# A list scheduler that repeats its pass, maxima spread through DRAM, and a search that moves from ScalarE to VectorE

## The chip, the cores and the metric

The kernel runs on one core of a Trainium2 chip. The time of a run is the device time of the whole program in microseconds (us). TensorE (PE in the rows) multiplies matrices, VectorE (DVE), ScalarE (ACT) and GpSimd (POOL) work on tiles, SyncE (SP) issues nearly all DMAs. Each engine works through its own list of instructions in order; semaphores join the lists.

## The reference

Two independent parts, put side by side in the output (S = 2048 rows, D = 1024):

```python
# A: sliding-window attention, 32 heads of 32, window 256
qkv = x @ wqkv                                   # (S, 3 D)
scores = where(0 <= i - j < 256, q k^T / sqrt(32), -1e9)
a = (softmax(scores) @ v) @ wo
# B: Fourier mixing by given matrices
re, im = xb @ dft_hid_re.T, xb @ dft_hid_im.T
b = dft_seq_re @ re - dft_seq_im @ im
out = concatenate([a, b], axis=-1)               # (S, 2 D)
```

All arrays are float32.

## The kernel before

A float32 operand is divided by a power of two taken from its largest magnitude and split into two float16 halves, high by ScalarE and low by VectorE (`split`, L431 and L439; L1102 and L1103 for the cosine parts). Three float16 products (`PASSES`) stand for one float32 product. Most products are two by two block products in seven multiplications instead of eight (`seven`, `seven_parts`), whose block sums VectorE and GpSimd form (`summed`, L1076). A `seven` multiplies into the PSUM banks `m0` to `m3` and calls a hook after each of its parts; ScalarE copies its first product to a second bank (L1194).

The work in the order in which it is written down: the projections to q, k and v (`plan`: `plain_units`, `sum_unit`), through DRAM to attention; then 64 units (`units`): per half p of the second transform (real, imaginary) and half c of the rows, eight "x" units (xb times the hidden matrix) and eight "c" units (a pair of row blocks of the sequence matrix, here the cosine pair, times that); last the product with wo. Attention is a generator whose blocks (`s_step`: scores, mask, exponent, transpose by DMA, `v_step`: times v) are advanced by `tick` beside the other matmuls, six blocks apart (`LAG`).

Before an operand can be scaled, its largest magnitude is needed in every partition. A row maximum per partition comes from VectorE (`top`, L457) or, as a sum of magnitudes, from ScalarE (`mean`, L1002); `spread` reduces the columns to one (`topone`, L464). `scale_of` and `u_look` then bring it across the partitions: TensorE transposes the column, copied 128 times, into the PSUM bank `old` (L471, L1059), and VectorE reduces that (L473, L1061). Four small VectorE instructions make the scale and its inverse (L1065 to L1068). `u_load` loads a cosine pair into two of six `raw` tiles, `u_look` finds its scale, `u_parts` makes its parts in `st` tiles (four). The bank `old` has one buffer, and the third key block of the scores (L586) uses it too.

No order of instructions is written by hand. `op` records an operation with its engine, an assumed cost, what it reads and writes, and for a DMA the transfer and a delay. `Plan.close` gives each a due time: a TensorE operation is due at the sum of TensorE costs written down before it, another as early as its users need. `Plan.run` then plays the program once: whenever an engine is free it takes the ready operation that is due first. The order in which that happens is the program. VectorE and GpSimd share a port: an operation with `port=True` on one is assumed to wait while the other holds it (`lock`). SP's DMAs use eight semaphores in turn, so each issue waits until the DMA eight before it has landed.

x of part A is loaded in four quarters of four pieces: the first quarter's scale (`vc`) comes from `top`, the second quarter's (with the first, `vx`) from `mean` (`x_top`).

Of the kernel before, what the change touches and what calls it, by code (L numbers as in the profile page):

```python
# [20 lines left out]
P = 128  # L21
# [36 lines left out]
RX = 1.0  # L58
DOWNQ = 16.0 * DOWN
# [32 lines left out]
SEM = 0.034  # L92
DRAIN = 0.17
# [3 lines left out]
MARGIN = 0.0  # L97


class Plan:  # L100
# [68 lines left out]

    def run(self):  # L170
        self.close()
        events, ready, seq = [], {e: [] for e in TAIL}, 0
# [28 lines left out]
        def start(o, t):  # L201
# [27 lines left out]
        def pick(e, t):  # L229
# [16 lines left out]
            for item in skipped:  # L246
                heapq.heappush(h, item)
            if got is not None and e in near and t < CALM:
# [69 lines left out]
WIRE = 2.0  # L318
# [6 lines left out]
def turned(n):  # L325
    return (n * 0.22, WIRE + 0.3)

# [6 lines left out]
def fused_kernel(ctx: ExitStack, tc: tile.TileContext, xa, wqk, wv, wo, xb, wd, cs, out):  # L334
# [39 lines left out]
    ws = tc.dram_tile((8, P, 7 * 2 * CH), F16, name="ws")  # L374
    xhs = tc.dram_tile((NT, P, 2 * ND * P), F16, name="xhs")
# [76 lines left out]

    def top(key, view, rk, i, n):
# [13 lines left out]

    def scale_of(key, v, s, wk, down=2.0 ** -14, loose=False):
        t1 = tops.pop(key)
        pt = old_ring.new()  # L470
        op("PE", 0.12, lambda: nc.tensor.transpose(pt.t[:, :P], t1.t[:, 0:1].to_broadcast([P, P]), ident),  # L471
           r=[(t1, 0), "ident"], w=[pt], loose=loose)
        dve(0.285, lambda: nc.vector.tensor_reduce(v, pt.t[:, :P], axis=AX.X, op=ALU.max), r=[pt], w=[wk])  # L473
# [25 lines left out]
    def dkey(*a):  # L499
        return ("dram", *a)  # L500
# [26 lines left out]
    o_ring = att_ring("o", [P, QB * P], F32, 1)  # L527

# [521 lines left out]
    def u_look(n):  # L1050
        p = units[n][1]
        key = f"u{n}"
        for j in range(2):
# [3 lines left out]
        t1 = tops.pop(key)  # L1057
        pt = old_ring.new()
        op("PE", 0.12, lambda: nc.tensor.transpose(pt.t[:, :P], t1.t[:, 0:1].to_broadcast([P, P]), ident),  # L1059
           r=[(t1, 0), "ident"], w=[pt])  # L1060
        dve(0.285, lambda: nc.vector.tensor_reduce(v.t[:, 0:1], pt.t[:, :P], axis=AX.X, op=ALU.max), r=[pt], w=[v])  # L1061
# [473 lines left out]
    for r in range(4):  # L1535
        x0, c0 = 16 * r, 16 * r + 8
        for j in range(8):
# [158 lines left out]
```

## Time and profile before

| | us |
|---|---|
| three runs | 1713.43, 1712.93, 1710.23 (median 1712.93) |
| profiled execution | 1711.95 |
| its span, first to last instruction | 1710.1 |
| TensorE busy | 1686.3 |
| VectorE busy | 1346.0 |
| ScalarE busy | 1134.5 |
| GpSimd busy | 668.9 |

The profile is of one execution. A row of the groups view gives line, engine, operation, tiles and count, then busy us and mean ns of one, then the idle time of the engine ahead of it and what ended it. A row of the waits view gives who waited for whom, total us, times, longest us. A row of the timeline gives start and length in us. Matmuls overlap, so their shown lengths are longer than their distance. `reg<-...` and the like name tiles without their buffer numbers. Mean share of the DMA engines is 82.9% of the span for the hardware queue.

### The profile page before, as it was taken

The page shows a single profiled execution, that of the slowest core. Times are in us where ns is not written, and L with a number is a line of the kernel's source. Part 1 is how long each engine was busy: PE and PEld are TensorE (multiplying, and loading weights), DVE is VectorE, ACT ScalarE, POOL GpSimd, SP SyncE. Part 2 cuts the span into 40 slices and gives each one's busy share as a digit, 9 for nine tenths or more (in the row PEclk, how much of TensorE's full clock was granted, in tenths as well). Part 3 has the DMA queues.
Part 4 walks back from the last instruction along what each step waited for, and adds up shares of the span by engine and source line. Part 5 has one row for each costly group of instructions (what it writes and reads, how often), then busy time and mean ns, then how long its engine had stood idle before and what let it go on. Part 6 is the DMA issues. An engine that isn't in the chain of part 4 may idle for free.

```text
span 1710.1 us, 31789 instructions
## 1 busy us (share of the span) xinstructions
PE 1686.3 (99%) x11607; PEld 909.7 (53%) x11607; DVE 1346.0 (79%) x2294; ACT 1134.5 (66%) x1934; POOL 668.9 (39%) x723
## 2 busy tenths in 40 slices
PE   8999999999999999999999999999999999999998
PEld 3446787675445455555455555555555555544443
DVE  6978997677987887776899886899885788879641
ACT  7656635666777898877786667887775786553321
POOL 0133500213434654424545564566553545611000
PEclk9999999999999999999999999999999999999999
DMA  6389799999999589999589998879999859973331
GB/s 264 119 323 339 226 311 278 251 238 238 232 258 256 124 200 245 210 251 237 119 195 282 247 283 187 176 163 233 262 249 227 162 129 218 228 263 111 111 99 74
DMA packets 469917, 368.35 MB, mean 215 GB/s; under 512 B 341760, under 2 KB 412416, under 8 KB 469760
## 3 DMA queue, kind: packets, MB, share of 16 engines
q1 hardware_dynamic: 468896, 363.17, 82.9%
q0 software_dynamic: 864, 3.15, 1.1%
q8 instruction: 91, 1.49, 0.4%
q14 instruction: 66, 0.54, 0.1%
HBM read 195.97 MB, written 96.86 MB: 171 GB/s over the span
## 4 chain that ended last, share of the span: by engine, by line
PE 85%; DVE 6%; ACT 4%; DMA 3%; issue 2%; SPq 0%; DVEq 0%; ACTq 0%
PE m L721 75%; PE pv L663 4%; PE s L586 3%; PE old L586 1%; DMA raw<-in_wd_dram 1%; ACT st L1102 1%; PE m L1324 1%; DMA qk<-qs 1%; DVE reg L439 1%; ACT s L612 1%; DVE top L457 1%; DVE reg L436 1%; DVE hl L436 1%; DVE mx L602 0%; DVE st L1103 0%
## 5 line engine op out<-in xcount | busy, mean ns | idle before, releaser
L721 PE MATMUL m<-reg,st 128*128 128x512 f16 x4776 | 1098.2, 379 | 9.0 <-ACT m L1194 4.6
L721 PEld LDWEIGHTS <-st 128*128 128x128 f16 x5400 | 512.3, 98 | 569.1 <-issue 13.9
L627 POOL TENSOR_SCALAR_AFFINE_SELECT z<-t 128x512 f16<-128x512 f16 x224 | 170.0, 766 | 382.2 <-PE pv L663 220.2
L1076 POOL TENSOR_TENSOR raw<-raw,raw 128x512 f32<-128x512 f32 x128 | 176.8, 1382 | 278.1 <-DVE st L1103 262.9
L612 ACT ACTIVATE s<-s,bias,escs 128x256 f32<-128x256 f32 (+1 forms) x512 | 270.7, 529 | 13.9
L436 DVE TENSOR_TENSOR hl<-s,hl 128x512 f16<-128x512 f32 (+1 forms) x256 | 170.8, 668 | 73.6 <-ACT hl L432 72.7
L606 ACT ACTIVATE bias<-mx,pshift,escs 128x2 f32<-128x2 f32 x256 | 98.3, 384 | 185.6 <-DVE mx L602 185.1
L630 POOL TENSOR_SCALAR_AFFINE_SELECT t<-t 128x512 f16<-128x512 f16 x224 | 180.6, 814 | 7.6
L602 DVE TENSOR_REDUCE mx<-s 128x2 f32<-128x512 f32 (+1 forms) x256 | 170.9, 668 | 3.2
L432 ACT ACTIVATE hl<-s 128x512 f16<-128x512 f32 (+1 forms) x256 | 146.7, 577 | 6.7 <-DMA t<-hl 4.6
L721 PEld LDWEIGHTS <-reg 128*128 128x128 f16 x1212 | 116.0, 98 | 63.0 <-issue 0.3
L1103 DVE SCALAR_TENSOR_TENSOR st<-raw,sc,st 128x1024 f16<-128x1024 f32 x96 | 130.0, 1357 | 16.0 <-ACT st L1102 15.3
L586 PEld LDWEIGHTS <-qk 96*128 96x128 f16 x1056 | 95.8, 98 | 84.9 <-issue 7.8
L1102 ACT ACTIVATE st<-raw,sc 128x1024 f16<-128x1024 f32 x96 | 109.5, 1142 | 36.0 <-PE m L721 26.2
L597 DVE COPY_PREDICATED s<-upper,old 128x256 f32<-128x256 uint32 x224 | 94.6, 422 | 45.5 <-PE old L586 22.6
L721 PE MATMUL m<-reg 128*128 128x512 f16 x480 | 114.1, 379 | 0.0
L1513 DVE SCALAR_TENSOR_TENSOR ybig<-m,fu,ybig 128x512 f32<-128x512 f32 x112 | 83.1, 743 | 23.2 <-PE m L721 21.9
L721 PE MATMUL m<-xz,st 128*128 128x512 f16 x432 | 97.3, 379 | 2.5 <-ACT m L1194 2.5
L586 PE MATMUL s<-qk,qk 96*128 96x128 f16 (+1 forms) x608 | 96.3, 253 | 3.3 <-DVE hl L436 3.2
L663 PE MATMUL pv<-vt,t 128*128 128x65 f16 x1984 | 98.1, 185 | 1.0 <-DVE o L674 1.0
L663 PEld LDWEIGHTS <-t 128*128 128x128 f16 x1984 | 88.0, 96 | 8.6 <-issue 1.1
L1002 ACT ACTIVATE junk<-raw 128x1024 uint8<-128x1024 f32 x82 | 85.9, 1048 | 4.2 <-DMA raw<-in_cs_dram 4.0
(172 smaller groups left out, 2132.2 us busy)
## 6 DMA issues: line engine op xcount, KB each, us to landing
raw<-in_cs_dram SPq DMA_DIRECT2D x64, 512.0 KB, 5.4
qk<-qs SPq DMA_DIRECT2D x192, 128.0 KB, 4.2
out_dram<-ybig SPq DMA_DIRECT2D x44, 512.0 KB, 5.2
qs<-ybig SPq DMA_DIRECT2D x64, 256.0 KB, 3.9
raw<-in_xb_dram SPq DMA_DIRECT2D x32, 512.0 KB, 5.5
raw<-in_wd_dram SPq DMA_DIRECT2D x32, 512.0 KB, 6.4
ybig<-out_dram SPq DMA_DIRECT2D x32, 512.0 KB, 5.0
vs<-ybig SPq DMA_DIRECT2D x32, 260.0 KB, 4.8
```

What stands on the lines that cost most here:

```text
L432: else nc.scalar.activation(dst(), src(), AF.Copy), r=r, w=w)
L436: op("DVE", c_dve(n), lambda: nc.vector.tensor_tensor(dst(), src(), hi(), op=ALU.subtract), r=r, w=w, port=port)
L586: nc.tensor.matmul(dst(j, a, e), qu.t[:, h, i * P:i * P + P], ku.t[:, h, ka:ke], start=True, stop=True, skip_group_check=True)
L602: dve(c_dve(2 * w), lambda: nc.vector.tensor_reduce(mx.t, sv(), axis=AX.X, op=ALU.max, negate=True), r=[(S, 0), (S, 1)], w=[mx])
L612: op("ACT", 0.32 + 0.00085 * w, lambda h=h: nc.scalar.activation(sv()[:, h], sv()[:, h], AF.Exp, bias=bias.t[:, h:h + 1], scale=es), r=[bi ...
L627: op("POOL", 0.637, lambda: nc.gpsimd.affine_select(out=z.t, in_=pk(), compare_op=ALU.is_gt, fill=0.0, base=0, pattern=[[0, 4], [-1, P]], ...
L630: op("POOL", 0.637, lambda: nc.gpsimd.affine_select(out=pk(), in_=pk(), compare_op=ALU.is_ge, fill=0.0, base=0, pattern=[[0, 4], [1, P]], ...
L663: nc.tensor.matmul(pvt()[:, r, j, lo:], lhs, vt.t[:, k % QB, at + lo:at + VW], start=a, stop=e, skip_group_check=True)
L721: nc.tensor.matmul(ps.t[:, j * n:j * n + n], lhs(), rhs(), start=first, stop=last, skip_group_check=True)
L1076: lambda: e.tensor_tensor(o(), a(), b(), op=ALU.subtract if sub else ALU.add), r=r, w=w, port=True)
L1102: op("ACT", c_act(n), lambda: nc.scalar.activation(dst(0), src(), AF.Copy, scale=scl()), r=[*r, sk_], w=wh)
L1103: op("DVE", c_dve(n, True), lambda: nc.vector.scalar_tensor_tensor(dst(1), src(), scl(), dst(0), op0=ALU.mult, op1=ALU.subtract), r=[*r, s ...
```

## The change

Five parts. (1) `run` plays the program 40 times (`forward`, the old pass) and keeps the order with the earliest planned end. After each pass `learn` looks for planned gaps on TensorE of 0.05 us or more, follows the operation behind the gap back through the predecessor that finished last, as far as 40 us, and makes each operation of another engine on that way due earlier by the gap, 3 us at most. (2) The assumed wait for the shared port is shorter (`SHARED`), and VectorE, about to take an operation that would wait for GpSimd's hold of the port, takes another from among its ready ones that needs no port and fits into the wait. (3) The maxima of the hidden matrices, of wo and of all cosine pairs but the last two cross the partitions by two DMAs: the column goes to a row of a DRAM tile (`rows`), and that row comes back into all partitions (`row`, three buffers), where VectorE reduces it. The last two pairs and all other operands keep the transposing matmul. (4) The second quarter of x is searched by VectorE too. (5) The assumed delay of a DMA is 1.9 us instead of 2.0, of a DMA transpose of n blocks 0.18 n + 1.5 instead of 0.22 n + 2.3, and cosine pairs are loaded and searched at earlier hooks.

```diff
+FAR = ("wd00", "wd01", "wd10", "wd11", "wo")
+SHARED = {"DVE": 0.18, "POOL": 0.14}
+SLIP = 0.3
+TRIALS = 40
+REACH = 40.0
+BOOST = 1.0
...
+    def learn(self, order):
+        clock, n = 0.0, 0
+        for o in [o for o in order if o.eng == "PE"]:
+            gap, clock = o.at - clock, o.at + o.cost
+            if gap < 0.05:
+                continue
+            x, seen = o, set()
+            while x is not None and x.at > o.at - REACH:
+                if x.eng not in ("PE", None) and x not in seen:
+                    x.due -= min(gap, 3.0) * BOOST
+                    n += 1
+                seen.add(x)
+                x = max(x.pre, key=lambda y: (y.fin, y.n), default=None)
+
     def run(self):
         self.close()
+        best = None
+        for i in range(TRIALS):
+            order = self.forward()
+            end = max(o.fin for o in order)
+            if best is None or end < best[0]:
+                best = end, order, [(o, o.at, o.fin) for o in order]
+            self.learn(order)
+        for o, at, fin in best[2]:
+            o.at, o.fin = at, fin
+        return best[1]
+
+    def forward(self):
...
-                cost += max(0.0, lock[other] - t)
+                cost += max(0.0, lock[other] - t - SHARED[e])
...
+            if got is not None and e == "DVE" and got.port:
+                wait = lock["POOL"] - t - SHARED[e]
+                if wait > 0.05:
+                    skipped = []
+                    while h and len(skipped) < 12:
+                        item = heapq.heappop(h)
+                        o = item[2]
+                        skipped.append(item)
+                        if not o.port and o.cost < wait + SLIP and not any(not b.has and room[b.ring] == 0 for b in gate.get(o, ())):
+                            skipped.pop()
+                            skipped.append((got.due, got.n, got))
+                            got = o
+                            break
...
-WIRE = 2.0
+WIRE = 1.9
...
 def turned(n):
-    return (n * 0.22, WIRE + 0.3)
+    return (n * 0.18, 1.5)
...
+    rows = tc.dram_tile((64, P), F32, name="rows")
...
+    def across(t1, v, wk, far, loose=False):
+        if not far:
+            pt = old_ring.new()
+            op("PE", 0.12, lambda: nc.tensor.transpose(pt.t[:, :P], t1.t[:, 0:1].to_broadcast([P, P]), ident),
+               r=[(t1, 0), "ident"], w=[pt], loose=loose)
+            dve(0.285, lambda: nc.vector.tensor_reduce(v(), pt.t[:, :P], axis=AX.X, op=ALU.max), r=[pt], w=[wk])
+            return
+        i = nrow[0] = nrow[0] + 1
+        pt = row_ring.new()
+        op("SP", C_ISSUE, lambda: nc.sync.dma_start(rows[i].rearrange("(p o) -> p o", o=1), t1.t[:, 0:1]), r=[(t1, 0)],
+           w=[dkey("row", i)], dma=(0.15, WIRE))
+        op("SP", C_ISSUE, lambda: nc.sync.dma_start(pt.t, rows[i].partition_broadcast(P)), r=[dkey("row", i)], w=[pt],
+           dma=(0.2, WIRE))
+        dve(0.285, lambda: nc.vector.tensor_reduce(v(), pt.t, axis=AX.X, op=ALU.max), r=[pt], w=[wk])
...
+        across(tops.pop(key), lambda: v, wk, key in FAR, loose)
...
-        if c:
-            mean(f"x{c // 2}", b, c % 2 * 4 + i, 1.0)
-        else:
-            top(f"x{c // 2}", v, b, c % 2 * 4 + i, 8)
+        top(f"x{c // 2}", v, b, c % 2 * 4 + i, 8)
...
+        across(tops.pop(key), lambda: v.t[:, 0:1], v, not (p == 1 and units[n][2] == 1 and units[n][3] > LAST))
...
-            lead = (m - 2, 0) if j > 1 else (c0 - 3 + 2 * j, 0)
+            lead = (m - 3, 4) if j > 2 else (c0 - 3 + 2 * j, 0) if j < 2 else (c0 - 1, 1)
             do(*lead, u_load, m, 1)
             do(*lead, u_load, m, 0)
-            look = (m - 2, 5) if j > 1 else (c0 - 3 + 2 * j, 1)
+            look = (m - 2, 1) if j > 2 else (c0 - 3 + 2 * j, 1) if j < 2 else (c0, 0)
```

All 40 passes run while the program is built, so they cost no device time. The new order differs on every engine. Three places follow.

TensorE before, among the first cosine pairs: the column `topone` of one pair is transposed into `old` between two products (`m_28`, `m_35`) of a unit.

```order
L721 LDWEIGHTS st_6854
L721 MATMUL m_28_6941<-reg_81,st_6854 128x512
L1059 MATMUL old_6961<-ident,topone_6955 128x128
L721 LDWEIGHTS st_6788
L721 MATMUL m_35_6911<-reg_81,st_6788 128x512
```

SP now, for such a pair: the column's write to `rows`, the read into `row` right behind it, then the transpose of attention tile `hl` and a load.

```order
L686 DMA_TRANSPOSE t_7382<-hl_7369 128x8x128
L1670 DMA out_dram<-ybig 128x1024
L530 DMA rows<-topone_7421 128x1
L532 DMA row_7465<-rows 128x128
L686 DMA_TRANSPOSE t_7473<-hl_7452 128x8x128
L467 DMA raw_7530<-in_wo_dram 128x1024
```

Of TensorE's list 35 of the 51 transposing matmuls are gone; SP's has 70 DMAs more.

VectorE now, for the same pair: the reduction of `row`, the four small instructions of the scale, then the mask of a score tile (`s`), a low half of another pair (`st`) and one of attention (`hl`).

```order
L739 TENSOR_TENSOR o_7334<-pv_7439,rs_7461 128x2x64
L534 TENSOR_REDUCE sc_7493<-row_7465 128x1
L1123 TENSOR_SCALAR sc_7493<-sc_7493 128x1
L1124 TENSOR_SCALAR sc_7493<-sc_7493 128x1
L1125 RECIPROCAL sc_7493<-sc_7493 128x1
L1126 TENSOR_SCALAR fu_7506<-fa,sc_7493 128x1
L662 COPY_PREDICATED s_7495<-upper,old_7500 128x2x128
L1161 SCALAR_TENSOR_TENSOR st_7491<-raw_6908,sc_7132,st_7491 128x1024
L486 TENSOR_TENSOR hl_7512<-s_7432,hl_7512 128x512
```

The reduction reads SBUF and waits for a DMA, where it read PSUM and waited for TensorE.

ScalarE before, near the start: between the high halves of x's first quarter (`reg_82` with scale `vc`) and of the first weights (`st_212`) stand the searches (`junk`) of x's second quarter (`top_156`).

```order
L431 ACTIVATE reg_81<-reg_82,vc 128x1024
L431 ACTIVATE st_212<-reg_81,scw 128x1024
L431 ACTIVATE reg_81<-reg_82,vc 128x1024
L1002 ACTIVATE junk,top_156<-reg_82 128x1024
L431 ACTIVATE reg_81<-reg_82,vc 128x1024
L1002 ACTIVATE junk,top_156<-reg_82 128x1024
L431 ACTIVATE reg_81<-reg_82,vc 128x1024
```

ScalarE now, at the same place:

```order
L481 ACTIVATE reg_81<-reg_82,vc 128x1024 x2
L481 ACTIVATE st_225<-reg_81,scw 128x1024
L1064 ACTIVATE junk,top_199<-reg_81 128x1024
L481 ACTIVATE reg_81<-reg_82,vc 128x1024 x2
L481 ACTIVATE st_246<-reg_81,scw 128x1024
```

One search, of weights, is left among the conversions. VectorE now searches x's second quarter (`top_155`) around the low halves of the next weights (`st_291`, `st_298`), and makes x's second scale `vx` behind two more searches (`top_356`):

```order
L508 TENSOR_REDUCE top_155<-reg_82 128x1 x2
L489 SCALAR_TENSOR_TENSOR st_291<-reg_81,scw,st_291 128x1024
L489 SCALAR_TENSOR_TENSOR st_298<-reg_81,scw,st_298 128x1024
L508 TENSOR_REDUCE top_155<-reg_82 128x1 x2
L489 SCALAR_TENSOR_TENSOR ybig<-m_1_233,ybig 128x512
L515 TENSOR_REDUCE topone_343<-top_155 128x1
L489 SCALAR_TENSOR_TENSOR ybig<-m_1_276,ybig 128x512
L515 TENSOR_REDUCE topone_351<-top_264 128x1
L515 TENSOR_REDUCE topone_353<-top_310 128x1
L508 TENSOR_REDUCE top_356<-raw_223 128x1
L508 TENSOR_REDUCE top_356<-raw_229 128x1
L526 TENSOR_REDUCE vx<-old_367 128x1
```

Before, those searches were ScalarE's, and on VectorE `vx` followed its `topone` directly.

More of the change, by code (lines that the diff above doesn't have):

```diff
@@ L247, in pick @@
                 heapq.heappush(h, item)
+            if got is not None and e == "DVE" and got.port:
[11 more added lines that the diff above has]
+                            break
+                    for item in skipped:
+                        heapq.heappush(h, item)
             if got is not None and e in near and t < CALM:
@@ L466, in spread @@
         tops[key] = c
-    def scale_of(key, v, s, wk, down=2.0 ** -14, loose=False):
[L469 to L473, printed above, removed]
+    nrow = [0]
+    def across(t1, v, wk, far, loose=False):
[12 more added lines that the diff above has]
+        dve(0.285, lambda: nc.vector.tensor_reduce(v(), pt.t, axis=AX.X, op=ALU.max), r=[pt], w=[wk])
+    def scale_of(key, v, s, wk, down=2.0 ** -14, loose=False):
+        across(tops.pop(key), lambda: v, wk, key in FAR, loose)
         def rest():
@@ L527, in fused_kernel @@
     o_ring = att_ring("o", [P, QB * P], F32, 1)
+    row_ring = att_ring("row", [P, P], F32, 3)
     def attention():
@@ L1056, in u_look @@
         v, f = sc_ring.new(), fu_ring.new()
[L1057 to L1061, printed above, removed]
+        across(tops.pop(key), lambda: v.t[:, 0:1], v, not (p == 1 and units[n][2] == 1 and units[n][3] > LAST))
         def rest():
```

## The prediction

> **What bounds the kernel now.** I read the page's busy shares first, then the stretches, then TensorE's waits. The first line gives busy us, share and count for each engine; the second is the granted TensorE clock in 40 slices.
>
> ```profile
> PE 1686.3 (99%) x11607; PEld 909.7 (53%) x11607; DVE 1346.0 (79%) x2294; ACT 1134.5 (66%) x1934; POOL 668.9 (39%) x723
> PEclk9999999999999999999999999999999999999999
> ```
>
> TensorE works through all of the 1710.1 us span, at full clock, so a saving elsewhere counts only where TensorE waits for it, and a TensorE instruction removed counts in full. Busy TensorE is not yet dense TensorE. The groups view gives a 512-column matmul 379 ns, while the chain of waits shows 754 matmuls end to end in 163.07 us, 0.216 us from start to start:
>
> ```profile
> L721 PE MATMUL m<-reg,st 128*128 128x512 f16 x4776 | 1098.2, 379 | 9.0 <-ACT m L1194 4.6
> 1539.39 163.07 PE m L721 x754
> ```
>
> So each pause is shown 0.16 us too short (379 less 216 ns). TensorE's waits, first in 0 to 100 us, then in 100 to 1540 us (total us, times, longest):
>
> ```profile
> PE m L721 <- ACT m L1194: 1.9, 1, 1.9
> PE m L1305 <- DVE reg L1300: 1.3, 1, 1.3
> PE m L721 <- DVE reg L439: 1.1, 2, 0.6
> PE m L721 <- ACT st L431: 0.9, 2, 0.6
> PE m L721 <- DVE st L439: 0.7, 1, 0.7
> PE m L721 <- DVE topone L464: 0.7, 1, 0.7
> ...
> PE m L721 <- ACT m L1194: 5.3, 5, 2.0
> PE s L586 <- DVE hl L436: 3.2, 7, 1.0
> ...
> PE old L1059 <- DVE topone L464: 0.6, 1, 0.6
> ```
>
> In the first 100 us, without the 1.3 us before any matmul can run, that is 5.3 us in 7 waits, 6.4 us with 0.16 added to each. From 100 to 1540 us all rows of the answer (five short ones left out here) add to 12.1 us in 18 waits, 15.0 us corrected. One of these waits does more harm than its length:
>
> ```profile
> 593.78 0.27 PE L1059 MATMUL old<-ident,topone 128*128 128x128 f32 x1
> 595.46 0.59 ACT L1194 ACTIVATE m<-m 128x512 f32<-128x512 f32 x1
> 596.10 1.07 PE L721 MATMUL m<-reg,st 128*128 128x512 f16 x4 [2.05 <-ACT m L1194]
> 597.39 3.36 PE L721 MATMUL m<-reg,st 128*128 128x512 f16 x8
> 600.59 0.27 PE L471 MATMUL old<-ident,topone 128*128 128x128 f32 x1
> 600.70 1.67 PE L721 MATMUL m<-reg,st 128*128 128x512 f16 x7
> ...
> 590.00:605.00 15.00, 12.95 (x80) 6.35 (x79) 12.53 (x33) 13.57 (x28) 1.20 (x2) 0.89 0.38 95
> ```
>
> TensorE stands until the PSUM copy of ACT (L1194), which is queued behind other ACT work, ends; then eight matmuls take 0.42 us each instead of 0.216, 1.6 us more, and the stretch's granted clock is 0.89 (last row; third number from the end). All that any schedule could win is thus 6.4 + 15.0 + 1.6 = 23 us.
>
> **The change, part by part.** *Thirty-five maxima leave TensorE.* The five keys in FAR and 30 of the 32 cosine pairs no longer use the transposing matmul into bank `old`. Two rows above price it: it starts at 600.59 and the next matmul at 600.70, 0.11 us. 35 x 0.11 = 3.85 us leave TensorE's stream. Nothing can take that back but a new wait.
>
> *In their place come two dependent DMAs each.* SP gets 70 more issues; at 0.43 us that is 30 us:
>
> ```profile
> L417 SPq DMA_DIRECT2D reg<-in_xa_dram x8: 328/428/997, 1.3 to 9.1; - x8
> out_dram<-late SPq DMA_DIRECT2D x4, 256.0 KB, 2.0
> ...
> qk<-qs SPq DMA_DIRECT2D x23, 128.0 KB, 4.4
> t<-hl SPq DMA_TRANSPOSE x35, 4.5
> ```
>
> No row has a 512-byte transfer. The nearest (us from issue to landing) are 2.0 at the quiet end of the kernel and 4.4 in 620 to 760 us, so a write and a read take 4.0 to 8.8 us; I take 8, because most pairs run in the loaded stage. Where the matmul path stood, one pair from 710 us on shows the time already spent:
>
> ```profile
> 710.02 0.14 DVE L464 TENSOR_REDUCE topone<-top 128x1 f32<-128x2 f32 x1
> 717.68 0.28 DVE L1061 TENSOR_REDUCE sc<-old 128x1 f32<-128x128 f32 x1
> 720.79 0.20 DVE L1068 TENSOR_SCALAR fu<-fa,sc 128x1 f32<-128x1 f32 x1
> 721.05 0.71 ACT L1102 ACTIVATE reg<-raw,sc 128x512 f16<-128x512 f32 x1
> ```
>
> The maximum waited 7.5 us for its spreading, with nothing pressing: the trip fits in that. The loads and `u_look` also move three to four of a unit's seven products earlier. That the scale has time is seen in who waits (first three rows), and loaded data is rarely late (the two groups):
>
> ```profile
> ACT st L1102 <- PE m L721: 34.3, 21, 5.4
> ACT st L1102 <- DVE sc L1067: 5.0, 3, 4.3
> POOL z L627 <- PE pv L663: 220.2, 60, 15.1
> ...
> L1002 ACT ACTIVATE junk<-raw 128x1024 uint8<-128x1024 f32 x82 | 85.9, 1048 | 4.2 <-DMA raw<-in_cs_dram 4.0
> L457 DVE TENSOR_REDUCE top<-raw 128x1 f32<-128x1024 f32 x48 | 57.3, 1208 | 2.4 <-DMA raw<-in_wd_dram 1.5 <-DMA raw<-in_xa_dram 0.8
> ```
>
> The cosine parts wait for a free stationary tile, which TensorE releases, far longer than for a scale; and POOL waits 220 us for pv to release masked tiles, so transposes that SP issues 2 or 3 us later, behind a read that waits for its write, reach no matmul. The danger is VectorE: `sc<-row` stands in its queue, as the order shows, directly ahead of the mask copy of the next score block, whose tile TensorE reuses. The planner gives each hop 1.9 us beyond issue and transfer; the loaded row has 4.4 in all for 128 KB, which the planner puts at 2.75 on an empty bus, so a trip can be 3.3 us later than planned. 35 x 3.3 = 115 us of VectorE standing, if none of the queueing is in the plan; the bounds for TensorE are 0 (its idle time, 1710 - 1346 = 364 us, takes it up) and 12 us (one tenth comes through). I take +2.5, near 0, because of the two groups above.
>
> The Trainium skill (DMA: Bandwidth & Descriptors, Anatomy of one DMA) gives a DMA a fixed part of about 2 us, nearly all of it waiting for the confirmation of the write. By that the trip would be about 4.9 us with two issues, as planned, this term 0 and the sum 2.5 us lower. The loaded rows above do not agree, the quiet one does.
>
> *x's second quarter is searched by VectorE.* ACT loses four searches of 1.04 us, VectorE gains four of 1.21 (row above):
>
> ```profile
> 21.81 0.61 PE L721 MATMUL m<-reg,st 128*128 128x512 f16 x2 [0.31 <-ACT st L431]
> 22.70 1.04 ACT L1002 ACTIVATE junk<-reg 128x1024 uint8<-128x1024 f32 x1
> 22.99 1.28 DVE L439 SCALAR_TENSOR_TENSOR reg<-reg,vc,reg 128x1024 f16<-128x1024 f32 x1
> 28.32 1.24 PE L721 MATMUL m<-reg,st 128*128 128x512 f16 x5 [0.62 <-DVE reg L439]
> 30.26 0.61 PE L721 MATMUL m<-reg,st 128*128 128x512 f16 x2 [0.59 <-ACT st L431]
> 31.58 0.61 PE L721 MATMUL m<-reg,st 128*128 128x512 f16 x2 [0.71 <-DVE topone L464]
> ```
>
> ACT's searches of x stood between the four conversions that TensorE waited for. Without them VectorE yields a piece every 1.28 us, and the six matmuls of a piece take 1.30. ACT has the first weights near 22.1 (the trace's first product starts at 21.81, and one more piece now goes ahead); VectorE's weights and three pieces follow, and the last piece's matmuls: 22.1 + 4 x 1.28 + 1.30 = 28.5, instead of 28.32 + 1.24 - 0.16 = 29.4. The waits of 0.59 and 0.71 (0.75 and 0.87 corrected) then go too, since the next weights are converted by 28.5: together -2.5. Against it the searches now stand on VectorE ahead of x's second scale, whose first use I expect some 1 us late. Net -1.5; bounds -6.4 (all early waits) and +1.2 (one search more ahead of a fill).
>
> *The repeated pass, the port rule and the new DMA costs* change only order. `learn` pulls forward the latest non-TensorE ancestor of each planned gap, and an ACT copy like the one at 595.46 is just that. Which of the 15.0 + 1.6 us were planned gaps and which came from wrong costs no row tells. The bounds are -16.6 (all goes) and, since nothing excludes a worse order, +5 (waits a third longer). I take -6, somewhat over a third, because L1194 is the largest releaser (5.3 of 12.1). A transpose now counts 4.2 us in the plan instead of 5.3; the row has 4.5, and no pv stands among TensorE's waits for one, so that costs nothing. Filling VectorE's port waits is worth nothing by itself, with VectorE at 79%.
>
> Sum from the profiled execution: 1711.95 - 3.85 + 2.5 - 1.5 - 6 = 1703.1 us. It was 1.0 us under the median of 1712.93, within the runs' spread, so I say 1703.5.
>
> **The rivals.** *Slower: VectorE stands for the rows.* Each late row holds VectorE in front of a mask copy, and `PE s <- DVE hl`, already the second wait, grows. Five pauses of 2.2 us, each with the 1.6 us of half clock seen at 597, cost 19.0 instead of 2.5: 1719.6. It decides from three such pauses on (11.4 against a gain of 11.35). For it: the trip's spread of 4.0 to 8.8. Against: loads are late by only 4.2 and 2.4 us in all.
>
> By the Trainium skill (TensorE: Matmul & The Clock Gate, HAM oscillation) the clock falls only after an idle window of some 3.4 us; pauses of 2.2 us would then cost no clock and this rival 1711.6. The trace has the fall after a pause of 2.2 us.
>
> *No change: the waits are not the plan's.* The order is new but pauses as often: 1711.95 - 3.85 + 2.5 = 1710.6.
>
> *Much faster: nearly all goes.* Early waits -4, later ones -13, trips free: 1711.95 - 3.85 - 17 = 1691.1.
>
> **How the numbers follow.** Chances: forecast 0.56, much faster 0.12, no change 0.17, slower 0.15. 0.2% (3.4 us) is what a measurement can tell: below 1709.5 is faster, above 1716.4 slower. The forecast and the much faster case and 0.02 of the third give faster 0.70; same takes 0.15 of the third and 0.02 of the slower case, 0.17; slower 0.13. The forecast's own range is 1696 to 1709; to leave out 2 in 10 it must reach to the no-change case and touch the slower one: 1693 to 1715.
>
> **What would show it.** Right: 16 transposing matmuls instead of 51; TensorE's waits from 100 to 1540 us under 9 us; no dip of the clock after 10 us; `sc<-row` waiting for its DMA under 1 us each; no pv waiting for a transpose. Wrong: rows of `sc<-row` that wait 2 us or more for DMA with scores or parts behind them, or a new wait of TensorE for conversions at 43 to 50 us, where x's second scale is used first.

## The result, and the profile after

The changed kernel takes 1921.6 us (median of four runs, 1919.3 to 1926.1) against 1711.7 us beside it on the same chip: 1.123 times as long, 95% interval 1.121 to 1.125. The profiled execution spans 1919.7 us, 209.6 more than before.

From the page after, first the busy time of each engine, the granted TensorE clock in 40 slices, and the chain that ended last, by engine and by line. The listing gained lines: `mm` is now L786, scores L651, the mask L662, `lo` (low half) L486, the transposes of attention L686.

```profile
PE 1740.7 (91%) x11572; PEld 921.3 (48%) x11572; DVE 1345.9 (70%) x2298; ACT 1138.4 (59%) x1926; POOL 667.1 (35%) x723
PEclk9999999999989889899999998998898999999999
PE 47%; DMA 29%; DVE 10%; ACT 7%; issue 5%; SPq 1%; POOL 1%; ACTq 0%; POOLq 0%; DVEq 0%
PE m L786 42%; DMA rows<-topone 8%; DMA t<-hl 7%; DMA row<-rows 5%; DMA raw<-in_cs_dram 2%; PE pv L728 2%; DMA qk<-qs 2%; DMA vt<-vs 2%; DVE hl L486 2%; ACT s L677 1%; DVE mx L667 1%; PE s L651 1%; DVE st L1161 1%; ACT hl L482 1%; ACT junk L1064 1%
```

The 35 matmuls are gone (11607 to 11572), and yet TensorE is busy 54.4 us longer (1740.7 less 1686.3), because its clock falls in slice after slice; and it idles 179.0 us (1919.7 less 1740.7) where it idled 23.8. So 155.2 us of the loss are pauses, and 54.4 are, nearly all, matmuls run slowly after them: by the traces' clock records TensorE was busy 112.7 us at half clock, 3.4 before, and half of the difference is 54.7. The last row names the new links of the chain: the write of a column to DRAM, the read of it, and the attention transposes.

The DMA issues of the changed kernel (count, KB each, median us from issue to landing):

```profile
t<-hl SPq DMA_TRANSPOSE x288, 5.3
row<-rows SPq DMA_DIRECT2D x35, 64.0 KB, 5.7
rows<-topone SPq DMA_DIRECT2D x35, 0.5 KB, 11.2
```

The smallest transfer is the slowest of all that SP issues. A trip's two medians add to 16.9 us; the trace tells the landing of only 15 of the 35 writes and 16 of the 35 reads. Who waited for whom (total us, times, longest), over all engines and for TensorE, with one row of SP's waits last:

```profile
POOL z L692 <- DMA t<-hl: 339.3, 50, 20.4
...
DVE sc L534 <- DMA row<-rows: 104.8, 22, 10.7
PE s L651 <- DVE hl L486: 94.0, 33, 7.9
ACT hl L482 <- DMA t<-hl: 84.6, 24, 9.1
...
PE s L651 <- DMA qk<-qs: 30.6, 5, 10.6
PE pv L728 <- DMA vt<-vs: 13.1, 4, 6.0
...
SPq L532 <- DMA rows<-topone: 126.4, 21, 8.9
```

VectorE stands for the rows, with the low halves of attention behind it, and TensorE's scores stand for those. But that is not all: scores and pv also stand for loads (`qk`, `vt`) that were nobody's worry before, GpSimd's wait for transposes grew from 154.0 to 339.3 us, and ScalarE's from 4.6 to 84.6. Transfers that have nothing to do with the trip became late too. SP itself stands: before it can issue a read it waits for the write, 126.4 us in 21 waits, and whatever is behind the read in its queue, transposes and loads of attention among them, is issued that much later.

One pause in the timeline (start, length, engine, line, work, what ended the idle time ahead), then the stretch's busy time of each engine, granted clock, DMA share and GB/s:

```profile
681.59 0.52 SPq L530 DMA_DIRECT2D rows<-topone  x1
...
695.10 0.34 SPq L532 DMA_DIRECT2D row<-rows  x1
...
700.53 0.28 DVE L534 TENSOR_REDUCE sc<-row 128x1 f32<-128x128 f32 x1 [10.70 <-DMA row<-rows]
700.73 0.42 DVE L662 COPY_PREDICATED s<-upper,old 128x256 f32<-128x256 uint32 x1
701.06 0.68 DVE L486 TENSOR_TENSOR hl<-s,hl 128x512 f16<-128x512 f32 x1
...
701.79 0.59 PE L651 MATMUL s<-qk,qk 96*128 96x256 f16 x2 [7.92 <-DVE hl L486]
...
703.43 4.16 PE L786 MATMUL m<-reg,st 128*128 128x512 f16 x12
```

```profile
680.00:694.00 14.00, 13.83 (x90) 6.66 (x88) 7.30 (x13) 9.58 (x18) 8.27 (x10) 1.00 1.22 98
694.00:709.00 15.00, 7.21 (x48) 3.73 (x48) 6.60 (x16) 6.52 (x13) 2.47 (x3) 0.66 1.01 248
```

The write is issued at 681.59; the read, seven issues later in SP's queue, at 695.10, after SP has stood 8.0 us; the reduction runs at 700.53, 18.9 us after the write. VectorE stood 10.70 us for it with the mask and the low half queued behind, so TensorE stood 7.92 us and then ran twelve matmuls in 4.16 us (0.35 each, against 0.216). From 680 to 694 us, mostly while the write was under way, all DMA engines together moved 98 GB/s (the mean of this execution is 193).

### The profile page after: what moved, and what is told of

Same layout as the page of the kernel before. It is cut to its first block, busy times and chain, and to the rows that moved or that the text cites. A ratio compares the mean times of both kernels' runs of the same rounds, so it can differ in the third digit from the quotient of the medians.

```text
span 1919.7 us, 31784 instructions
## 1 busy us (share of the span) xinstructions
PE 1740.7 (91%) x11572; PEld 921.3 (48%) x11572; DVE 1345.9 (70%) x2298; ACT 1138.4 (59%) x1926; POOL 667.1 (35%) x723
## 4 chain that ended last, share of the span: by engine, by line
PE 47%; DMA 29%; DVE 10%; ACT 7%; issue 5%; SPq 1%; POOL 1%; ACTq 0%; POOLq 0%; DVEq 0%
PE m L786 42%; DMA rows<-topone 8%; DMA t<-hl 7%; DMA row<-rows 5%; DMA raw<-in_cs_dram 2%; PE pv L728 2%; DMA qk<-qs 2%; DMA vt<-vs 2%; DVE hl L486 2%; ACT s L677 1%; DVE mx L667 1%; PE s L651 1%; DVE st L1161 1%; ACT hl L482 1%; ACT junk L1064 1%
## 5 line engine op out<-in xcount | busy, mean ns | idle before, releaser
L786 PE MATMUL m<-reg,st 128*128 128x512 f16 x4776 | 1119.5, 388 | 10.3 <-DVE st L1161 4.2
L786 PEld LDWEIGHTS <-st 128*128 128x128 f16 x5400 | 520.6, 99 | 618.3 <-issue 52.2
L692 POOL TENSOR_SCALAR_AFFINE_SELECT z<-t 128x512 f16<-128x512 f16 x224 | 169.3, 768 | 624.3 <-DMA t<-hl 339.3
L1134 POOL TENSOR_TENSOR raw<-raw,raw 128x512 f32<-128x512 f32 x128 | 183.9, 1437 | 270.2 <-DVE st L1161 229.6
L486 DVE TENSOR_TENSOR hl<-s,hl 128x512 f16<-128x512 f32 (+1 forms) x256 | 170.9, 668 | 115.1 <-ACT hl L482 113.2
L651 PE MATMUL s<-qk,qk 96*128 96x128 f16 (+1 forms) x608 | 100.7, 260 | 132.6 <-DVE hl L486 94.0
L651 PEld LDWEIGHTS <-qk 96*128 96x128 f16 x1056 | 96.8, 99 | 217.5 <-issue 130.9
L695 POOL TENSOR_SCALAR_AFFINE_SELECT t<-t 128x512 f16<-128x512 f16 x224 | 171.1, 776 | 5.0
L786 PEld LDWEIGHTS <-reg 128*128 128x128 f16 x1212 | 118.8, 100 | 80.0 <-issue 19.9
L662 DVE COPY_PREDICATED s<-upper,old 128x256 f32<-128x256 uint32 x224 | 94.2, 421 | 74.5 <-PE old L651 47.6
L786 PE MATMUL m<-reg 128*128 128x512 f16 x480 | 123.1, 403 | 6.4 <-DVE reg L1571 6.4
L728 PEld LDWEIGHTS <-t 128*128 128x128 f16 x1984 | 92.3, 99 | 18.4 <-issue 15.5
L786 PE MATMUL m<-xz,st 128*128 128x512 f16 x432 | 96.7, 379 | 1.2 <-ACT m L1252 1.2
```

What stands on the lines that cost most here:

```text
L486: op("DVE", c_dve(n), lambda: nc.vector.tensor_tensor(dst(), src(), hi(), op=ALU.subtract), r=r, w=w, port=port)
L651: nc.tensor.matmul(dst(j, a, e), qu.t[:, h, i * P:i * P + P], ku.t[:, h, ka:ke], start=True, stop=True, skip_group_check=True)
L692: op("POOL", 0.637, lambda: nc.gpsimd.affine_select(out=z.t, in_=pk(), compare_op=ALU.is_gt, fill=0.0, base=0, pattern=[[0, 4], [-1, P]], ...
L695: op("POOL", 0.637, lambda: nc.gpsimd.affine_select(out=pk(), in_=pk(), compare_op=ALU.is_ge, fill=0.0, base=0, pattern=[[0, 4], [1, P]], ...
L728: nc.tensor.matmul(pvt()[:, r, j, lo:], lhs, vt.t[:, k % QB, at + lo:at + VW], start=a, stop=e, skip_group_check=True)
L786: nc.tensor.matmul(ps.t[:, j * n:j * n + n], lhs(), rhs(), start=first, stop=last, skip_group_check=True)
```

## Experiments

All expectations were written before the runs. "Beside it" is the kernel before on the same chip; every ratio is to that. Where a kernel adds transfers that nobody uses (write-only, read-only and their variants), the maxima still come by TensorE.

### Take the trips away

`e1_no_far` is the changed kernel with every maximum on the old path.

```diff
-        if not far:
+        if True:
```

> The changed kernel, with every maximum brought across by the transposing matmul again (51 instead of 16); the repeated pass, the port rule, the DMA costs, the earlier hooks and VectorE's search of x stay. Theory W (the writes: each write of 128 x 4 bytes lands after 11.2 us, holds up other transfers meanwhile, and VectorE, SP and then TensorE stand behind it): about 1705 us, 1697 to 1712. Rival T (any trip of two DMAs in the loaded stage is too long for in-order engines, the write is nothing special): the same, 1697 to 1712. Rival O (the new order itself is bad, from the repeated pass and the lower DMA costs, and the trips only show it): above 1800.

Measured: 1724.4 us, ratio 1.0081 (1.0065 to 1.0098). The trips cost 197 of the 210 us. The other 13 belong to the rest of the change, which the forecast had at a gain; none of the three expected times came out.

`e2_far_alone` puts only the trips into the kernel before (`across`, `FAR`, the tile `rows` and the ring `row` of the diff; old pass, old costs, old search).

> The kernel before, with only the 35 trips through DRAM; one planning pass, old port rule, old DMA costs, old hooks, ScalarE's search of x. Theories W and T: above 1850 us, rows landing after about 11 us, VectorE waiting about 100 us for them. Rival O: 1705 to 1715.

Measured: 1857.3 us, ratio 1.0855 (1.0829 to 1.0881). The trips alone lose 146 us, so it takes neither the repeated pass nor the new costs to make them harmful. VectorE's waits for the rows came to 70.0 us here, not to the 100 expected.

### The write or the read

`e5_write_only`: the kernel of `e1_no_far` issues the same 35 writes, and nothing reads the row or waits for it. `e6_read_only`: instead 35 reads of a 512-byte row of an input into all partitions.

```diff
+        if far:      # e5: the write, nobody waits for it
+            op("SP", C_ISSUE, lambda: nc.sync.dma_start(rows[i].rearrange("(p o) -> p o", o=1), t1.t[:, 0:1]), r=[(t1, 0)], ...)
+        if far:      # e6: a broadcast read
+            op("SP", C_ISSUE, lambda: nc.sync.dma_start(rw.t, xb[i % 16, 0, 0].partition_broadcast(P)), r=[(t1, 0)], w=[rw], ...)
```

> The first kernel of this set (all maxima by TensorE), with the 35 writes of a 128-value column to DRAM issued beside it; nobody reads them, no engine waits for one except for the semaphore eight DMAs later. Theory W: 1760 us or more, the writes landing after 9 us or more, and other transfers landing later too (transposes 5 us or more instead of 4.4). Rival T: at most 1715, writes landing after 4 to 5 us like other DMAs of that stage.

> The first kernel of this set, with 35 reads of one 512-byte DRAM row into all partitions issued beside it (a row of an input, so nothing was written to it), at the places of the writes; nobody uses them. Theory W: at most 1715 us, reads landing after 4 to 5 us. Rival T: the same. A third possibility, that the read of one row by all partitions is what holds up the queues: 1760 or more.

Measured: writes 1848.5 us, ratio 1.0803 (1.0750 to 1.0857); reads 1727.7 us, ratio 1.0097 (1.0077 to 1.0117). Beside 1724.4 the reads cost nothing clear of the noise; that they came out above the 1715 expected is the 13 us of the kernel under them. The 35 writes cost 124 us, 3.5 each, with no engine waiting for a row; SP, which must wait for the DMA eight before, stood 19.3 us for the writes. TensorE's largest wait there comes first below, then the waits for transposes in this kernel, then the same in `e1_no_far`.

```profile
PE s L655 <- DVE hl L486: 48.8, 21, 5.9
```

```profile
POOL z L696 <- DMA t<-hl: 355.7, 60, 17.0
ACT hl L482 <- DMA t<-hl: 84.3, 31, 7.0
```

```profile
POOL z L692 <- DMA t<-hl: 140.4, 38, 13.2
ACT hl L482 <- DMA t<-hl: 2.7, 3, 1.3
```

So most of the loss is not a wait for the trip. The writes make other transfers late. (The expected sign, transposes that land after 5 us or more at the median, cannot be read: the trace tells the landing of 39 of 288, with a median of 4.4 us.)

### What about the write

Three variants keep 35 writes of 128 pieces from SBUF. `e7_write_512` writes 512 bytes a piece (another tile's contents, 64 KB in all); `e8_write_apart` keeps four-byte pieces and sets each 512 bytes behind the one before; `e11_write_64`, `e19_write_32` and `e18_write_16` narrow that to 64, 32 and 16 bytes.

```diff
-    rows = tc.dram_tile((64, P), F32, name="rows")
+    rows = tc.dram_tile((64, P, P), F32, name="rows")        # e11: (64, P, 16), e19: (64, P, 8), e18: (64, P, 4)
-            ... nc.sync.dma_start(rows[i].rearrange("(p o) -> p o", o=1), t1.t[:, 0:1]) ...
+            ... nc.sync.dma_start(rows[i][:, 0:1], t1.t[:, 0:1]) ...        # e7: dma_start(rows[i], ident)
```

> As the run that only writes, but each of the 35 writes brings 512 bytes per partition (the identity tile, 64 KB in all) to a row of its own for each partition; nobody reads them. Theory S (the harm comes from pieces of 4 bytes, or from 128 of them in one 512-byte row): 1720 to 1730, landing after 4 to 5 us, no packet of another transfer over 3 us. Rival Q (any further write in this stage lands late and holds up the rest): above 1800.

> As the run that only writes, still 128 x 4 bytes, but each piece goes to a row of its own, 512 bytes from the next. If the harm comes from 128 pieces meeting in one 512-byte row: 1720 to 1730, landing after 4 to 5 us, few packets over 3 us. If it comes from a 4-byte piece as such: above 1800, landing after 9 us or more, several hundred packets over 3 us.

> The 35 unused writes of 128 four-byte pieces once more, each piece now 64 bytes behind the one before, so that eight of them share 512 bytes of DRAM and none shares 64. Theory B (pieces are merged in blocks of 512 bytes, one after the other): still several us a write and a time between 1728 and 1848, near 1740 if the harm goes with the number of pieces that share a block (8 of 128). Theory C (the block is 64 bytes or less): 1724 to 1730 and landings near 3.8 us, as with 512 bytes between them.

> The same, 32 bytes apart (two share 64 bytes). If pieces collide that share 64 bytes: slower than the 1723.7 of 64 bytes, 1730 to 1770. If the block is 32 bytes or less: 1722 to 1730.

> The 35 unused writes, their 128 pieces of four bytes 16 bytes apart (four share 64 bytes). If pieces collide that share 64 bytes: some landings of 6 us or more and a time of 1735 to 1800. If only neighbours in a smaller block collide: 1722 to 1730 and landings near 3.8 us.

| write of 128 pieces | us | ratio (interval) | median landing, us |
|---|---|---|---|
| none (`e1_no_far`) | 1724.4 | 1.0081 (1.0065 to 1.0098) | |
| 4 bytes, end to end | 1848.5 | 1.0803 (1.0750 to 1.0857) | 11.7 |
| 4 bytes, every 16 | 1721.2 | 1.0060 (1.0041 to 1.0080) | 4.2 |
| 4 bytes, every 32 | 1726.2 | 1.0090 (1.0064 to 1.0115) | 4.2 |
| 4 bytes, every 64 | 1723.7 | 1.0069 (1.0051 to 1.0086) | 3.6 |
| 4 bytes, every 512 | 1727.6 | 1.0094 (1.0073 to 1.0114) | 3.8 |
| 512 bytes, end to end | 1728.3 | 1.0098 (1.0078 to 1.0118) | 3.9 |

Of these only the four-byte pieces laid end to end do harm. Their 11.7 us is the median of three landings, all that the trace of `e5_write_only` tells; in the other rows it is that of all 35. It is not the size of a piece, nor an extra write, nor a share of a 64-byte block: two and four pieces per 64 bytes are harmless, which the expectation of `e19_write_32` and `e18_write_16` had open. The line that issues the write, in the write-only kernel and then with pieces 512 bytes apart:

```profile
L524 SPq DMA_DIRECT2D rows<-topone x35: 320/439/1269, 334.3 to 1583.4; - x35
...
DMA to landing us min/median/max: 8.0/11.7/13.2
```

```profile
L524 SPq DMA_DIRECT2D rows<-topone x35: 319/432/1308, 334.9 to 1470.1; - x35
...
DMA to landing us min/median/max: 1.4/3.8/6.5
```

SP issues both equally fast, every engine of both kernels has the same instructions in the same order, and both move 474957 packets by their pages, so the pieces are as many: the difference arises behind the issue. Counted in the traces, no packet took over 3 us before, 371 did in the write-only kernel and 2 with the pieces 512 bytes apart (4 in `e1_no_far`); 344 of the 371 are packets of 4096 and 256 bytes, of other transfers. They lie where the writes are: 370 of the 371 overlap the 16 us behind the issue of a write, and all 35 writes have some. From 1.5 to 10 us behind those issues all DMA engines together moved 101 GB/s, and 185 with the pieces 512 bytes apart. Whether the place is the memory or the DMA engines, and why 16 bytes are far enough, no run shows; distances between 4 and 16 bytes were not tried.

### The trip without the pile-up

The writes explained 124 of 197 us. Is the rest the price of waiting for any two DMAs? `e14_trip_apart` is the changed kernel with write, dependent read and reduction, but pieces 512 bytes apart; the read takes the first piece's row (the rest of it blanked by a 64 KB write), so only one partition's maximum comes back.

```diff
+        for j in (1, 2, 3, 4) if i == 1 else (i + 3,):
+            op("SP", C_ISSUE, lambda j=j: nc.sync.dma_start(rows[j], ident), r=["ident", (t1, 0)], w=[dkey("blank", j)], ...)
-        ... dma_start(rows[i].rearrange("(p o) -> p o", o=1), t1.t[:, 0:1]) ...
+        ... dma_start(rows[i][:, 0:1], t1.t[:, 0:1]) ...
-        ... dma_start(pt.t, rows[i].partition_broadcast(P)) ...
+        ... dma_start(pt.t, rows[i][0].partition_broadcast(P)) ...
```

> The changed kernel with its 35 trips as they are, write, dependent read, reduction by VectorE, but the 128 pieces of each write 512 bytes apart; the read takes the row of the first piece (blanked ahead by a 64 KB write, a kind shown to be harmless), so only the first partition's maximum comes back. Theory P (the two dependent DMAs are cheap once the pieces do not collide, as the prediction had it): within 6 us of the 1724.4 of the kernel with all maxima by TensorE, so 1718 to 1730, and reductions that wait under 1 us each. Theory V (VectorE stands for any such trip in front of the scores): 1740 to 1795, with waits of 2 us or more for the row and the scores behind them.

Measured: 1718.9 us, ratio 1.0054 (1.0038 to 1.0069): below the 1724.4 without trips by 5.5 us, with intervals that just touch. Its landings and its waits:

```profile
row<-rows SPq DMA_DIRECT2D x35, 64.0 KB, 4.2
rows<-topone SPq DMA_DIRECT2D x35, 0.5 KB, 4.0
```

```profile
DVE sc L536 <- DMA row<-rows: 10.3, 8, 3.1
...
PE s L653 <- DVE hl L486: 6.0, 8, 2.0
```

With 8.2 us for a trip VectorE waits 10.3 us in all instead of 104.8, and the scores hardly at all. SP's wait for the write, 126.4 us in the changed kernel, is 4.6 here. To wait for a trip is cheap here; the remaining 73 us went with the late landing of this write, for which SP and VectorE stood, and of what it held up. How they divide between SP and VectorE no run shows.

### The other 13 us: what the plan believes of a DMA

`e9_old_costs` gives `e1_no_far` the DMA costs of before; `e10_one_pass` keeps the new costs and takes the first pass's order; `e12_one_pass_old_costs` does both.

```diff
-WIRE = 1.9                      # e9, e12
+WIRE = 2.0
-    return (n * 0.18, 1.5)      # e9, e12
+    return (n * 0.22, WIRE + 0.3)
-TRIALS = 40                     # e10, e12
+TRIALS = 1
```

> The changed kernel with all maxima by TensorE (1724 us) and the planner's old DMA costs (2.0 us, and 0.22 n + 2.3 for transposes). Theory M (the lower costs let the plan put transfers' users too early; this is where 13 us went): 1704 to 1714. Rival L (the repeated pass fits its order too closely to its own costs): 1720 to 1728. Rival X (search of x by VectorE, hooks, port rule): the same, 1720 to 1728.

> The changed kernel with all maxima by TensorE (1724 us) and one planning pass instead of 40. Rival L: 1704 to 1714. Theory M: 1720 to 1730. Rival X: 1720 to 1730.

> All maxima by TensorE and the DMA costs of before (the kernel that gave 1710.2), with the order of the first pass instead of the best of 40. If repeating the pass is worth about what it was worth at the lower costs (4.5 us): 1713 to 1717. If it only fits the order to the plan's own numbers: 1708 to 1712.

| all maxima by TensorE | 40 passes | one pass |
|---|---|---|
| delay 1.9, transposes 0.18 n + 1.5 | 1724.4, 1.0081 (1.0065 to 1.0098) | 1728.9, 1.0105 (1.0088 to 1.0122) |
| delay 2.0, transposes 0.22 n + 2.3 | 1710.2, 0.9995 (0.9985 to 1.0004) | 1710.7, 0.9997 (0.9986 to 1.0007) |
| delay 2.6, transposes 0.22 n + 2.9 | 1703.3, 0.9966 (0.9952 to 0.9979) | 1712.0, 1.0005 (0.9996 to 1.0014) |

Undoing the costs takes away the whole 13 us; repeating the pass did not cause them. In the trace of `e1_no_far` TensorE's longest pause looks like this. First the waits, then the timeline:

```profile
ACT junk L1064 <- DMA raw<-in_cs_dram: 22.9, 13, 7.1
DVE topone L515 <- ACT junk L1064: 16.7, 11, 5.7
...
PE s L651 <- DVE hl L486: 8.5, 6, 5.5
```

```profile
1146.32 0.33 SPq L467 DMA_DIRECT2D raw<-in_cs_dram  x1
...
1147.26 10.20 SPq L686 DMA_TRANSPOSE t<-hl  x2
...
1157.57 1.06 ACT L1064 ACTIVATE junk<-raw 128x1024 uint8<-128x1024 f32 x1 [7.12 <-DMA raw<-in_cs_dram]
...
1159.93 0.15 DVE L515 TENSOR_REDUCE topone<-top 128x1 f32<-128x2 f32 x1 [5.68 <-ACT junk L1064]
...
1162.73 0.58 PE L651 MATMUL s<-qk,qk 96*128 96x256 f16 x2 [5.48 <-DVE hl L486]
```

It is the same chain of waits as with the trip, without one: the search that uses a load stands ahead of attention's work on ScalarE, the load is late, and ScalarE and VectorE stand for it with the scores behind them. But this load is late by far more than the plan's numbers moved: it landed 11.2 us after its issue (the median of its kind here is 5.7), while two transposes behind it held SP for 10.20 us and the DMA engines moved 44 GB/s from 1154 to 1158 us. What slowed them is not shown, nor how much of the 13 us such pauses make up. With the costs of before (`e9_old_costs`) the first of the waits is a twelfth:

```profile
ACT junk L1064 <- DMA raw<-in_cs_dram: 1.9, 3, 1.4
```

Then the other direction: a longer delay than before, with 40 passes (`e13_higher_costs`), with one (`e16_higher_costs_one_pass`), and in the kernel before, alone (`e15_before_higher_cost`).

```diff
-WIRE = 2.0      # of the kernel before; e13 and e16 also take its formula for a transpose
+WIRE = 2.6
```

> All maxima by TensorE, 40 passes, and the assumed delay of a DMA raised to 2.6 us (a transpose of n blocks 0.22 n + 2.9), where 2.0 gave 1710.2 and 1.9 with 0.18 n + 1.5 gave 1724.4. Theory M (TensorE waits for transfers that land later than planned, so a margin pays): 1698 to 1707, faster than the kernel before. Rival (the costs of before were already enough, and the waits left have other reasons): 1708 to 1714. Rival Q (later due times make buffers the limit): above 1714.

> The kernel of the higher costs (all maxima by TensorE, delay 2.6 us, 1703.3 with 40 passes), with the order of the first pass. If the margin pays only because the repeated pass repairs what it disturbs: 1709 to 1716, as the kernel before gives with the same margin (1713.7). If the margin pays together with the other parts (x searched by VectorE, the port rule, earlier hooks): 1701 to 1707.

> The kernel before with one number changed, the assumed delay of a DMA 2.6 us instead of 2.0. Theory M (the margin in the plan is what pays, whatever the rest): 1703 to 1708, faster than before by some 5 us. Rival (the margin pays only together with the repeated pass or with VectorE's search of x): within 0.2% of before.

Measured: 1703.3 us, ratio 0.9966 (0.9952 to 0.9979); 1712.0, ratio 1.0005 (0.9996 to 1.0014); 1713.7, ratio 1.0015 (1.0007 to 1.0024). In these runs the margin pays only together with the repeated pass. `e13_higher_costs` beats both kernels by its interval, but its nine runs fall into two groups, five of 1702.6 to 1703.3 and four of 1708.2 to 1710.1, for which I have no reason to show.

### The trips, made harmless, and the better plan together

`e17_trips_16` computes everything: pieces 16 bytes apart in four DRAM rows used in turn (each blanked once), the 2 KB read back into every partition, VectorE reducing every fourth element, delay 2.6.

```diff
-    rows = tc.dram_tile((64, P), F32, name="rows")
+    rows = tc.dram_tile((4, P, 4), F32, name="rows")
-        ... dma_start(pt.t, rows[i].partition_broadcast(P)) ...
+        ... dma_start(pt.t, rows[i].rearrange("p o -> (p o)").partition_broadcast(P)) ...
```

> The changed kernel whole, with two alterations: the pieces of a column's write lie 16 bytes apart (the row read back is 2 KB per partition, 256 KB in all, of which VectorE reduces every fourth element), and the planned DMA delay is 2.6 us (a transpose of n blocks 0.22 n + 2.9). Theory (adjoining pieces were the whole harm, the trip itself saves 35 x 0.11 us, and the margin pays with the repeated pass): 1697 to 1704, at or below the 1703.3 without trips. Rival (the 256 KB read lands too late, or the longer trip makes VectorE stand): 1706 to 1740.

Measured: 1709.9 us, ratio 0.9993 (0.9983 to 1.0003). The harm of the trips is gone (1709.9 against 1921.6), but the 1703 was not reached. One pause stands out in the profiled execution, which at 1715.55 us is the slowest of the eleven:

```profile
1425.44 6.51 SPq L753 DMA_TRANSPOSE t<-hl  x1
...
1433.01 0.60 ACT L482 ACTIVATE hl<-s 128x512 f16<-128x512 f32 x1 [6.61 <-DMA t<-hl]
...
1433.64 0.69 DVE L486 TENSOR_TENSOR hl<-s,hl 128x512 f16<-128x512 f32 x1 [7.97 <-ACT hl L482]
...
1434.39 0.59 PE L654 MATMUL s<-qk,qk 96*128 96x128 f16 x4 [7.71 <-DVE hl L486]
```

A transpose held SP for 6.51 us and ScalarE waited for it. The time is in the rival's range, but one of the rival's two reasons is not what happened: VectorE waited 2.1 us in all for the rows of the cosine pairs, and the 256 KB read landed after 5.1 us at the median. Whether that read made the transpose late or the new order placed it badly is open.

## Why the prediction was wrong, point by point

**The price of the trip is the step that failed.** "A write and a read take 4.0 to 8.8 us; I take 8": they took 11.2 and 5.7, 16.9 together. The bounds came from the nearest rows by bytes, a 256 KB store at the quiet end and 128 KB loads; what decided was how the pieces of the write lie in DRAM, of which no row of before had the like. For a write with pieces apart the same bounds hold well (4.0 + 4.2 in `e14_trip_apart`). The worst case of "115 us of VectorE standing" came near in size (104.8 us for `sc<-row`), but by luck: it was 35 times 3.3 us, and there are 22 waits of 4.8. And it is not so that "one tenth comes through": TensorE's wait for `hl` alone is 94.0; in `e5_write_only`, where there is no row to wait for, it is 48.8. That "transposes that SP issues 2 or 3 us later, behind a read that waits for its write, reach no matmul" failed with the price: SP's waits there are 6.0 us on average and up to 8.9, and TensorE came to wait for loads that SP issues. And a cost was missing from the list altogether: a DMA that slows others, which is 124 of the 197 us.

The Trainium skill (DMA: Bandwidth & Descriptors, Anatomy of one DMA), by which the trip would have been 4.9 us, does not hold for this trip, with 11.2 us for the write alone, nor quite for the one with its pieces apart, with 8.2. The section describes DMAs that GpSimd issues; SP issues these. The same page of the Trainium skill (Specifications) says that transfers under 512 bytes make the DMA engines read, modify and write; by itself that would condemn every four-byte piece, and the runs with 16 to 512 bytes between the pieces disagree (1721 to 1728 beside 1724).

**The rival "Slower: VectorE stands for the rows" had one of the mechanisms**, the chain from the row over VectorE to the scores, and its price was mis-sized: five pauses of 2.2 us, each with 1.6 us of half clock, where there are 33 waits for `hl` of 2.8 us on average and 54.4 us of slow matmuls. The slowing of other transfers it did not have. What the clock does after a short pause can be read in the changed kernel: TensorE's waits of 2.00 and 1.83 us that end at 1609.28 and 1626.52 are followed by a granted clock of 0.61 (first and second row below), and one of 2.73 us that ends at 1028.06 by full clock (third row).

```profile
1610.00:1614.00 4.00, 4.00 (x28) 1.65 (x24) 3.82 (x6) 3.93 (x8) 3.88 (x5) 0.61 1.05 136
1627.00:1631.00 4.00, 4.00 (x14) 1.45 (x11) 3.66 (x9) 3.34 (x7) 2.84 (x4) 0.61 0.63 80
1028.00:1033.00 5.00, 4.94 (x47) 2.79 (x47) 3.71 (x9) 2.81 (x7) 1.33 (x3) 1.00 1.08 273
```

The Trainium skill's rule on an idle window of some 3.4 us (TensorE: Matmul & The Clock Gate, HAM oscillation) does not agree with the first two.

**The 35 matmuls** left, worth 3.85 us, and "nothing can take that back but a new wait" is what happened. Where the new wait is nearly absent (`e14_trip_apart`), the kernel is 5.5 us faster than with them, about that size within the two intervals. At a delay of 2.6 it is the other way: 1709.9 with harmless trips, 1703.3 without. So the 3.85 us themselves are not shown.

**x's second quarter** agrees with what was worked out. TensorE's waits in the first 100 us after the change:

```profile
PE m L1363 <- DVE reg L1358: 1.3, 1, 1.3
PE m L786 <- ACT m L1252: 1.2, 1, 1.2
PE m L786 <- DVE st L489: 0.7, 1, 0.7
PE m L786 <- ACT st L481: 0.7, 1, 0.7
```

Without the first row that is 2.6 us in three waits, where it was 5.3 in seven: -2.7 instead of -1.5. The feared wait at 43 to 50 us does not appear. No run moves the search alone, so the other parts of the change may have their share in this.

**The repeated pass, the port rule and the new costs**, taken at -6 with +5 as the worst, were +13 (`e1_no_far`). The sentence that failed is the one on the costs: "The row has 4.5, and no pv stands among TensorE's waits for one, so that costs nothing." A lower planned delay does not act only where transfers are waited for today: with it ScalarE's waits for the cosine loads went from 1.9 to 22.9 us. Which of the two numbers did it, the delay or the transposes', was not separated. The -6 itself was within reach: with a delay of 2.6 the repeated pass gives 1703.3 us (1708 to 1710 in four of nine runs) where one pass gives 1712.0. At 2.0 it gives nothing (1710.2 and 1710.7).

**What would show it.** The 16 transposing matmuls came out right, and pv waits for no transpose. TensorE's waits from 100 to 1540 us, forecast under 9 us, hold 87.8 for `hl` alone; the clock dips; and `sc<-row` waits 4.8 us on average in 22 of its 30 reductions, the sign that was named for wrong. The limit of 23 us on any gain held: the best of all orders gained 0.34%, 5.8 us.

## What to carry to other kernels

Before a transfer is priced by its bytes, look at how its pieces lie at the destination, and ask what it does to other transfers: a 512-byte write of 128 adjoining pieces cost 3.5 us of the kernel without anybody waiting for it. A scheduler's planned delay is a safety margin as well as an estimate: an engine that works in order stands with everything behind it when a transfer is later than planned, so compare it with the loaded landing, and try it upwards as well as downwards; here upwards paid only with the repeated pass. And a change of several parts deserves one run with each part alone: here one part lost 197 us and another 13, and the parts that were right could not be seen.

## What was not expected of the hardware

A write of 512 bytes in 128 four-byte pieces end to end landed after 7.7 to 16.1 us (15 of 35 in the changed kernel) and held up unrelated packets; the same pieces 16 bytes apart landed after 4.2 us at the median and cost no time clear of the noise. Nor did a 512-byte row read into all 128 partitions, which landed after 4.4 us. And the issue of a transpose by DMA can hold SP's queue: in these rows (ns, least, median and most), before and after, the longest issue grows from 5.3 to 10.9 us, while the median goes from 1.23 to 1.27.

```profile
L621 SPq DMA_TRANSPOSE t<-hl x256: 1188/1233/5320, 267.3 to 1482.5; - x128
```

```profile
L686 SPq DMA_TRANSPOSE t<-hl x256: 1188/1271/10857, 263.7 to 1682.1; - x128
```
